# Layer norm of the second thousand tokens: features-by-tokens input in place of TensorE transposes

## The chip, the cores and the metric

One core of a Trainium2 chip runs the whole program. The metric is the device time of one execution in microseconds; the kernel before has a median of 2365.61 us over 3 runs (2364.18 to 2366.06). All tensors are float32.

## The reference

x has 2048 tokens of 1024 features. It is normalised over the features, xn = (x - mean) / sqrt(var + 1e-5), and xn feeds two branches. Branch A is linear attention with 32 heads of 32 features:

```python
xn = _layernorm(x, axis=-1)
s = _A_ref(xn, A_wqkv, A_w_phi, A_wo)      # softmax features, sums over the tokens, output product
g = _silu(_B_ref(xn, B_w1, B_w3, B_w2))    # silu(xn @ w1) * (xn @ w3) @ w2, 3584 hidden features
return x + s * g
```

TensorE sums over the partitions of both its operands, so every product with xn needs xn with features on the partitions, while mean and variance are per token and are easiest with tokens on the partitions.

## The kernel before, in words

**Products in three passes, seven for eight.** Every float32 operand is split into a high part (ScalarE casts, line 93) and a low part (VectorE subtracts, line 94), and a product takes three passes over the pairs. Blocks are multiplied by a scheme with seven products in place of eight: the activation operands are called A11, A12, A22, S1 to S4 (sums of blocks), the weight operands B11, B21, B22, T1 to T4.

**The stage in which the change lies.** The first stage multiplies w1 and w3 with the tokens: 28 column blocks of 128 features for the first 1024 tokens, then the same 28 for the second 1024 (loop over `seq`, lines 614 to 639). I call one of its products a step and number the steps as `seq` does: a step is 12 matmuls at line 627, and seven steps make a column block. Each step n does, in the order of the program: its matmuls; the weight sums on GpSimd that are due (lines 129 and 130, 553, 554); the split of the weight operand that step n+4 will need (ScalarE line 93, VectorE line 94, tile `bo`); whatever side work has been put at n (`after`); and then the eviction of its own result (`evict`, lines 563 to 592). Within this stage the five queues keep the program's order (`manual_schedule`), so that an instruction that waits holds all behind it on its queue.

**Evictions.** The seven steps of a block end in three PSUM banks' tags: `bankb` has three buffers, `banka` and `bankc` one each. In the single `bankc` S1 is started and copied out by ScalarE (line 576), S4 is added on top and evicted by VectorE (line 580, `wk<-bankc,wk`), and three steps later the next block's S1 starts in the same buffer: it can't start before that line 580 has ended. These steps are 84 (S4) and 87 (S1), 91 and 94, 98 and 101, and so on every seven.

**Side work.** Beside the steps the stage prepares what later stages need. `side_x` (four calls) makes the normalised operands of the second 1024 tokens, two 128-token tiles (a pair, numbers 4 to 7) at a time: it loads the two tiles with tokens on the partitions, takes mean and variance (`stats`, lines 193 to 196; `rstd`, 199 to 209), normalises them in place (`norm`, 211 to 214, VectorE), turns each of the four halves with four TensorE transposes (`turn`, 216 to 220), copies the turned half out of PSUM on ScalarE (`raw_x`, 222 to 225), forms the block sums on GpSimd (`a_sums`, 227 to 237), and splits and stores seven operands (`store_quad`, tiles `xoA` and `xoS`, DRAM tensors `xo_d1`). `side_fold` multiplies weight blocks by w_phi on TensorE (tile `pw`), `side_kv` prepares the weights of the key, value and query products (tiles `wkv`, `wkvo`), nine calls from step 69 on, 11 steps apart. Which step a piece stands at is worked out when the kernel is built: `room(step, cost)` goes on from a step until the VectorE time that the steps' own work and the pieces already placed there take stays within 2.4 us. GpSimd work isn't counted there. Side work that comes first takes its room first: `side_x`, then the folds, then `side_kv`.

**Queues.** All loads and stores of this stage are issued by SyncE (SP), in order.

Of the kernel before, what the change touches and what calls it, by code (L numbers as in the profile page):

```python
# [8 lines left out]
F = mybir.dt.float32  # L9
# [8 lines left out]
P = 128  # L18
NT = S // P
# [6 lines left out]


@with_exitstack
def tile_kernel(ctx: ExitStack, tc: tile.TileContext, x, wkT, wqT, wv, wphi, wo, w1, w3, w2, out):
    nc = tc.nc  # L30
    open_pools = {}

# [35 lines left out]
    dram = ctx.enter_context(tc.tile_pool(name="dram", bufs=1, space=DRAM))  # L68
# [15 lines left out]
    kv_d = [dram.tile([P, 8, DH], F, name=f"kv_d{c}") for c in range(2)]  # L84
    kvu_d = dram.tile([P, 16, DH], F, name="kvu_d")
    z_d = dram.tile([1, 2, 4, 4, 2, DH], F, name="z_d")


    PASSES = ((0, 0), (0, 1), (1, 0))
# [85 lines left out]
    def blk(name):  # L175
        return xp.tile([P, 4, P], F, name=name, tag="x")

    def flat(t):
        return t.rearrange("p k t -> p (k t)")
# [7 lines left out]
    def load_x(t, halves):  # L187
        for h in range(2):
            nc.sync.dma_start(halves[h], x[t * P:(t + 1) * P, h * 512:(h + 1) * 512])
        return halves  # L190

    def stats(mv, j, xt):
        st = small.tile([P, 2, 6], F, name="st")
        for a in range(2):
            nc.vector.bn_stats(st[:, a, :], xt[a])
        nc.vector.bn_aggr(mv[:, j], st.rearrange("p a b -> p (a b)"))

    def rstd(mv):

        sd = small.tile([P, 4, 2], F, name="sd")  # L200
        var = mv[:, :, 1]
        nc.scalar.activation(sd[:, 0], var, AF.Sqrt, bias=eps_t)
        nc.vector.reciprocal(sd[:, 1], sd[:, 0])

        nc.vector.tensor_mul(sd[:, 2], sd[:, 1], sd[:, 1])
        nc.vector.scalar_tensor_tensor(sd[:, 3], var, EPS, sd[:, 2], op0=OP.add, op1=OP.mult)
        nc.vector.tensor_scalar(sd[:, 3], sd[:, 3], -0.5, 1.5, op0=OP.mult, op1=OP.add)
        nc.vector.tensor_mul(sd[:, 1], sd[:, 1], sd[:, 3])
        return sd

    def norm(mv, sd, j, xt):

        for a in range(2):
            nc.vector.tensor_scalar(xt[a], xt[a], mv[:, j, 0:1], sd[:, 1, j:j + 1], op0=OP.subtract, op1=OP.mult)

    def turn(half):
        pt = ps.tile([P, 4, P], F, name="pt", tag="tr", bufs=3)
        for k in range(4):
            nc.tensor.transpose(pt[:, k, :], half[:, k * P:(k + 1) * P], ident)  # L219
        return pt  # L220

    def raw_x(pt):
        xf = blk("xf")
        nc.scalar.copy(xf, pt)
        return xf

    def a_sums(a, eng, part=None):

        if part in (None, 0):
            a["S3"] = blk("s3")  # L230
            eng.tensor_sub(flat(a["S3"]), flat(a["A11"]), flat(a["A21"]))
            a["S1"], a["S2"], a["S4"] = a["A21"], a["A11"], a["A12"]
            eng.tensor_add(flat(a["S1"]), flat(a["A21"]), flat(a["A22"]))
        if part in (None, 1):
            eng.tensor_sub(flat(a["S2"]), flat(a["S1"]), flat(a["A11"]))
        if part in (None, 2):
            eng.tensor_sub(flat(a["S4"]), flat(a["A12"]), flat(a["S2"]))
# [82 lines left out]
    for p in range(2):  # L320
        sd = rstd(mvs[p])
# [20 lines left out]
    for q in range(4):  # L342
        if q % 2 == 0:
            sd = rstd(mvs[2 + q // 2])
# [30 lines left out]
    before, after, rooms = {}, {}, []  # L375
# [10 lines left out]
    def at(step, f, d=after):  # L386
        d.setdefault(step, []).append(f)
# [4 lines left out]
    def room(step, cost):  # L392

        while True:
            f, j = divmod(step - 3, 7)
            base = (0.7, 0.7, 1.4, 1.4, 2.1, 0.7, 1.4 if f % 2 == 0 else 2.1)[j]
            if base + took.get(step, 0) + cost <= 2.4:
                took[step] = took.get(step, 0) + cost
                return step
            step += 1  # L400

    def store_quad(step, d, src, name):

        step = room(step, 1.0)

        def f():
            t = qp.tile(list(src().shape[:1]) + [2] + list(src().shape[1:]), R, name=name, tag="q")
            split(t[:, 0], t[:, 1], src())
            at(step + 2, lambda: nc.sync.dma_start(d, t.bitcast(F)))
        at(step, f)  # L410
        return step

    def side_x(i, s0):
        xt, a, mv, sd, pts = [], {}, [], [], {}
        t0, t1 = pairs[i]

        def load():
            xt.extend(load_x(t, [flat(blk("xt")) for _ in range(2)]) for t in (t0, t1))
            mv.append(small.tile([P, 2, 2], F, name="mv", bufs=4))

        at(s0, load)
        at_ = s0 + 2
        for j in range(2):
            at_ = room(at_ + 1, 1.6)
            at(at_, lambda j=j: stats(mv[0], j, xt[j]))
        at_ = room(at_ + 1, 1.0)
        at(at_, lambda: sd.append(rstd(mv[0])))
        for j in range(2):
            at_ = room(at_ + 1, 1.0)
            at(at_, lambda j=j: norm(mv[0], sd[0], j, xt[j]))  # L430
        s1 = at_ + 1
        for m, (n, j, hf) in enumerate((("A11", 0, 0), ("A12", 0, 1), ("A21", 1, 0), ("A22", 1, 1))):
            at(s1 + m, lambda n=n, j=j, hf=hf: pts.update({n: turn(xt[j][hf])}), before)
            at(s1 + m, lambda n=n: a.update({n: raw_x(pts[n])}))
        at_ = s1
        for n in ("A11", "A12"):
            at_ = store_quad(at_ + 1, xo_d[1][n][:, i - 4], lambda n=n: a[n], f"xo{n}")
        at_ = max(at_ + 1, s1 + 7)
        for m in range(3):
            at(at_ + m, lambda m=m: a_sums(a, nc.gpsimd, m))  # L440
        at_ += 1
        for n in ("S3", "S1", "S2", "S4", "A22"):
            at_ = store_quad(at_ + 1, xo_d[1][n][:, i - 4], lambda n=n: a[n], f"xo{n}")
# [59 lines left out]
    for i in range(4, 8):  # L503
        side_x(i, FIRST_STEP + 16 * (i - 4))
# [109 lines left out]
    for step, (k, an) in enumerate(seq):  # L614
        if step == 4:
            in_order(ENG.PE, ENG.Activation, ENG.DVE, ENG.Pool, ENG.SP)
        tb, f = divmod(k, NF)
# [6 lines left out]
        n = 0  # L624
# [477 lines left out]
    for r, new in enumerate(steps):  # L1102
        kb, i = new or (NKB, 0)
# [41 lines left out]
        if 26 <= r < 34:  # L1145
            c, a = (r - 26) // 4, (r - 26) % 4
            nc.sync.dma_start(zr_d[32 * a:32 * a + 32, c], z_d[:, c, a].rearrange("o j s f -> o (j s f)").to_broadcast([32, 256]))
        if 8 <= r < 24:
            c, j, s = (r - 8) // 8, (r - 8) // 2 % 4, r % 2
# [195 lines left out]
```

## Time and profile before

| what | value |
|---|---|
| median of 3 runs | 2365.61 us (2364.18 to 2366.06) |
| profiled execution, span | 2365.9 us (its own time is given by this span alone) |
| TensorE busy (PE) | 2337.4 us, 99% |
| VectorE busy (DVE) | 1753.2 us, 74% |
| ScalarE busy (ACT) | 859.2 us, 36% |
| GpSimd busy (POOL) | 760.5 us, 32% |
| DMA moved | 586.83 MB, mean 248 GB/s |

The profiled execution lies 0.3 us above the median, inside the spread of the runs. The shares are averages over stages; the stage of the change is the first half of the program, and the side work of `side_x` lies between 75 and 320 us. In the views of the timeline a line gives the start, the duration, the engine, the source line, the operation, the tile written and the tiles read, and, in brackets, the idle time ahead of it with what ended it.

### The profile page before, as it was taken

What the parts mean: (1) busy time and instruction counts of PE and PEld (TensorE: products, weight loads), DVE (VectorE), ACT (ScalarE), POOL (GpSimd) and SP (SyncE); (2) the same over time, 40 slices, a digit from 0 to 9 for tenths busy, and PEclk for the clock granted to TensorE, in tenths of its full rate; (3) what the DMA queues carried; (4) which work ended last, traced back from release to release, by engine and by line L of the source; (5) the groups of instructions that cost most, each with busy time, mean ns of one, the idle gap of its engine ahead of it and who ended that gap; (6) DMA issues with size and microseconds to landing.
All of it is one profiled execution on the core that took longest, in us unless ns stands there. A gap on an engine that the chain in (4) does not pass through costs nothing.

```text
span 2365.9 us, 35878 instructions
## 1 busy us (share of the span) xinstructions
PE 2337.4 (99%) x13298; PEld 1925.0 (81%) x13298; DVE 1753.2 (74%) x2539; ACT 859.2 (36%) x1534; POOL 760.5 (32%) x569
## 2 busy tenths in 40 slices
PE   6999999999999999999999999999999999999999
PEld 5888888888888888888888788888888888888877
DVE  8567788775688888885576555798688778888883
ACT  6445554443354445443232111234422222243100
POOL 1233555442355555552000000241011111115872
PEclk9999999999999999999999999999999999999999
DMA  7667689877887778776998877999445443377753
GB/s 262 202 216 237 230 292 309 286 249 226 260 279 261 257 264 281 261 267 218 372 341 323 326 240 256 350 351 333 154 137 179 178 178 111 125 254 289 250 186 132
DMA packets 319406, 586.83 MB, mean 248 GB/s; under 512 B 25600, under 2 KB 158208, under 8 KB 316544
## 3 DMA queue, kind: packets, MB, share of 16 engines
q1 hardware_dynamic: 304448, 569.87, 69.9%
q10 hardware_dynamic: 14784, 14.68, 1.8%
q8 instruction: 105, 1.72, 0.3%
q14 instruction: 69, 0.57, 0.1%
HBM read 379.19 MB, written 205.79 MB: 247 GB/s over the span
## 4 chain that ended last, share of the span: by engine, by line
PE 95%; DMA 2%; DVE 2%; SPq 1%; issue 1%; ACT 0%; POOL 0%; ACTq 0%; POOLq 0%; DVEq 0%
PE bankb L627 25%; PE bankb L1083 13%; PE bankc L627 12%; PE bankb L679 11%; PE pm L1210 7%; PE bankc L1083 6%; PE banka L627 6%; PE bankc L679 5%; PE banka L1083 3%; PE banka L679 3%; PE po L1054 1%; PE pkv L665 1%; PE pw L248 1%; SPq L166 0%; PE pt L219 0%
## 5 line engine op out<-in xcount | busy, mean ns | idle before, releaser
L94 DVE TENSOR_TENSOR bo<-rw,bo 128x512 fp32r<-128x512 f32 x336 | 307.7, 916 | 151.4 <-ACT bo L93 149.3
L1093 POOL TENSOR_TENSOR acc<-acc,u 128x512 f32<-128x512 f32 x48 | 63.4, 1321 | 449.1 <-ACT u L1092 434.3
L93 ACT CAST bo<-rw 128x512 fp32r<-128x512 f32 x336 | 201.1, 617 | 4.5 <-DMA w_d0T<-w2o 2.4
L1083 PE MATMUL bankb<-bo,as 128*128 128x512 f32 x816 | 200.7, 389 | 0.0
L1083 PEld LDWEIGHTS bankb<-bo,as 128*128 128x128 f32 x816 | 153.1, 188 | 31.9 <-DVE acc L1095 0.2
L1210 PE MATMUL pm<-wos,oT 128*128 128x512 f32 x720 | 166.9, 390 | 0.0
L627 PE MATMUL bankb<-op0A,bo 128*128 128x512 f32 x672 | 164.0, 391 | 0.1
L627 PE MATMUL bankb<-op0S,bo 128*128 128x512 f32 x672 | 163.2, 391 | 0.0
L627 PE MATMUL bankc<-op0S,bo 128*128 128x512 f32 x672 | 162.9, 391 | 0.0
L627 PE MATMUL bankc<-op1S,bo 128*128 128x512 f32 x672 | 161.5, 389 | 1.0 <-ACT bo L93 1.0
L627 PE MATMUL bankb<-op1S,bo 128*128 128x512 f32 x672 | 161.6, 389 | 0.1
L627 PE MATMUL bankb<-op1A,bo 128*128 128x512 f32 x672 | 161.4, 389 | 0.0
L1210 PEld LDWEIGHTS pm<-wos,oT 128*128 128x128 f32 x720 | 134.6, 188 | 30.6 <-issue 2.9
L627 PEld LDWEIGHTS bankc<-op1S,bo 128*128 128x128 f32 x672 | 126.0, 188 | 27.6 <-ACT bo L93 1.4
L627 PEld LDWEIGHTS bankb<-op1S,bo 128*128 128x128 f32 x672 | 126.0, 188 | 26.7 <-ACT h L569 0.6
L627 PEld LDWEIGHTS bankb<-op1A,bo 128*128 128x128 f32 x672 | 126.1, 188 | 26.2
L627 PEld LDWEIGHTS bankb<-op0S,bo 128*128 128x128 f32 x672 | 125.6, 188 | 25.6
L627 PEld LDWEIGHTS bankc<-op0S,bo 128*128 128x128 f32 x672 | 125.5, 188 | 25.7
L627 PEld LDWEIGHTS bankb<-op0A,bo 128*128 128x128 f32 x672 | 125.4, 188 | 25.8 <-DVE op0A L94 0.4
L1083 PE MATMUL bankc<-bo,as 128*128 128x512 f32 x576 | 146.1, 389 | 0.0
L1095 DVE TENSOR_TENSOR acc<-bankb,acc 128x512 f32<-128x512 f32 x152 | 104.3, 686 | 30.8 <-PE bankb L1083 26.6
L1083 PEld LDWEIGHTS bankc<-bo,as 128*128 128x128 f32 x576 | 108.1, 188 | 22.4
(246 smaller groups left out, 4686.7 us busy)
## 6 DMA issues: line engine op xcount, KB each, us to landing
rw<-in_w SPq DMA_DIRECT2D x224, 256.0 KB, 3.5
hr<-h_d SPq DMA_DIRECT2D x56, 512.0 KB, 4.1
xoS<-xo_d0S SPq DMA_DIRECT2D x48, 512.0 KB, 8.7
xoS<-xo_d1S SPq DMA_DIRECT2D x48, 512.0 KB, 6.6
xoA<-xo_d0A SPq DMA_DIRECT2D x36, 512.0 KB, 7.2
xoA<-xo_d1A SPq DMA_DIRECT2D x36, 512.0 KB, 6.2
e<-e_d SPq DMA_DIRECT2D x32, 512.0 KB, 5.6
h_d<-h SPq DMA_DIRECT2D x56, 256.0 KB, 4.0
```

The costliest lines, as they stand in the source:

```text
L93: nc.scalar.copy(hi, src)
L94: (by or nc.vector).tensor_sub(lo, src, hi.bitcast(F))
L248: nc.tensor.matmul(pw[:, g, :], wr[:, g], bd[:, 4 * c + g, :], start=True, stop=True)
L627: nc.tensor.matmul(bank, bt[:, w, kk], aos[tb][an][:, u, kk], start=an in ("A11", "A12", "S1") and n == 0, stop=LAST[b] == an and n == 11, ...
L665: nc.tensor.matmul(pkv[sl, m], e[:, m // 4, (m % 4) * P + 32 * h:(m % 4) * P + 32 * h + 32], v[:, 4 * (m % 4) + h], start=first and m == 0 ...
L679: nc.tensor.matmul(bank[b], xo[an][:, u, k], wb[bn][:, w, k], start=an in ("A11", "A12", "S1") and n == 0, stop=LAST[b] == an and n == 11, ...
L1054: nc.tensor.matmul(po[a][32 * j:32 * j + 32, 256 * c:256 * c + 256], kvt[sl, c, j, s], ets[c, j // 2][sl, 2 * (j % 2) + s].rearrange("p t ...
L1083: nc.tensor.matmul(bank[b], t[:, u, pos + k], bos[kb, bn, k][:, w], start=first and n == 0, stop=LAST[b] == an and n == 5, skip_group_chec ...
L1093: nc.gpsimd.tensor_add(c, c, u)
L1095: nc.vector.tensor_add(c, pb, c)
L1210: nc.tensor.matmul(p, oT[a][k // 4][:, u, k % 4], wos[c, 4 * (k % 2) + k // 2][:, w], start=n == 0, stop=n == 23)
```

## The change

For pairs 4 to 7 x is given to the kernel a second time, laid out by the host as an input `xT` with features on the partitions (for each of the 8 tiles of 128 tokens, 128 partitions of 2 x 4 x 128 numbers). The tokens-by-features load and the statistics stay. Normalising and turning are replaced: mean and factor of the pair are put side by side in `mv`, stored to DRAM as four rows of 128 numbers (`st_d`), read back to all 128 partitions (`rows`, 2 KB each), and four blocks of `xT` are loaded straight into the tiles that `raw_x` filled before. GpSimd subtracts the mean row from each (`centre`), VectorE multiplies by the factor row (`scale_x`). `norm`, `turn` and `raw_x` aren't called for these pairs any more. The first 1024 tokens are as before.

```diff
-        xt, a, mv, sd, pts = [], {}, [], [], {}
+        xt, a, mv, sd, rows = [], {}, [], [], []
         t0, t1 = pairs[i]
+        d = st_d[i - 4]
...
-        at(at_, lambda: sd.append(rstd(mv[0])))
-        for j in range(2):
-            at_ = room(at_ + 1, 1.0)
-            at(at_, lambda j=j: norm(mv[0], sd[0], j, xt[j]))
-        s1 = at_ + 1
-        for m, (n, j, hf) in enumerate((("A11", 0, 0), ("A12", 0, 1), ("A21", 1, 0), ("A22", 1, 1))):
-            at(s1 + m, lambda n=n, j=j, hf=hf: pts.update({n: turn(xt[j][hf])}), before)
-            at(s1 + m, lambda n=n: a.update({n: raw_x(pts[n])}))
-        at_ = s1
+
+        def root():
+            sd.append(rstd(mv[0]))
+            nc.vector.tensor_copy(mv[0][:, :, 1], sd[0][:, 1])
+
+        at(at_, root)
+        at(at_ + 1, lambda: nc.sync.dma_start(d.rearrange("o j m p -> p (o j m)"), mv[0].rearrange("p j m -> p (j m)")))
+
+        def load_t():
+            rows.append(blk("rows"))
+            nc.sync.dma_start(flat(rows[0]), d.rearrange("o j m p -> o (j m p)").to_broadcast([P, 512]))
+            for n, t, hf in (("A11", t0, 0), ("A12", t0, 1), ("A21", t1, 0), ("A22", t1, 1)):
+                a[n] = blk("xf")
+                nc.sync.dma_start(flat(a[n]), xT[t - NT // 2][:, hf].rearrange("p k t -> p (k t)"))
+
+        at(at_ + 4, load_t)
+        s1 = at_ + 7
+        for m, (n, j) in enumerate((("A11", 0), ("A12", 0), ("A21", 1), ("A22", 1))):
+
+            def centre(n=n, j=j):
+                nc.gpsimd.tensor_sub(a[n], a[n], rows[0][:, 2 * j].unsqueeze(1).to_broadcast([P, 4, P]))
+
+            def scale_x(n=n, j=j):
+                nc.vector.tensor_mul(a[n], a[n], rows[0][:, 2 * j + 1].unsqueeze(1).to_broadcast([P, 4, P]))
+
+            at(s1 + m, centre)
+            at_ = room(max(at_ + 1, s1 + m + 1), 0.7)
+            at(at_, scale_x)
+        s1 = at_ - 3
```

The pieces that follow (splits, sums, stores of the pair) move with it, and the pieces of `side_kv`, which take the room that is left, move as well. By the rules of `room` pair 7 has its last split at step 99 in place of step 90. Source lines after the added ones are higher in the new kernel: line 94 is 95 there, 580 is 602, 553 and 554 are 575 and 576, 129 to 130 are 130 to 131.

On VectorE, the 12 rows from the eviction of step 84 on. In these rows `bo` is the split for a later step, `xoS` a stored operand of pair 7, `wkvo` one of `side_kv`, `wk`, `h` the step's own evictions. Before:

```order
L580 TENSOR_TENSOR wk_851<-bankc,wk_851 128x512
L581 TENSOR_TENSOR h_855<-h_855,wk_851 128x512
L94 TENSOR_TENSOR bo<-rw,bo 128x512
L94 TENSOR_TENSOR xoS_2907<-s_2833,xoS_2907 128x512
L94 TENSOR_TENSOR bo<-rw,bo 128x512
L585 TENSOR_TENSOR wk_850<-wk_850,wk_852 128x512
L589 TENSOR_TENSOR wk_849<-wk_849,wk_850 128x512
L94 TENSOR_TENSOR bo<-rw,bo 128x512
L94 TENSOR_TENSOR xoS_2949<-xf,xoS_2949 128x512
L94 TENSOR_TENSOR bo<-wk_853,bo 128x512
L94 TENSOR_TENSOR xoS_2971<-xf,xoS_2971 128x512
L94 TENSOR_TENSOR bo<-rw,bo 128x512
```

The same place in the new kernel, where `xf<-xf,rows` is `scale_x`:

```order
L602 TENSOR_TENSOR wk_855<-bankc,wk_855 128x512
L603 TENSOR_TENSOR h_859<-h_859,wk_855 128x512
L95 TENSOR_TENSOR bo<-rw,bo 128x512
L452 TENSOR_TENSOR xf<-xf,rows 128x512
L95 TENSOR_TENSOR wkvo<-wkv,wkvo 128x512
L95 TENSOR_TENSOR bo<-rw,bo 128x512
L607 TENSOR_TENSOR wk_854<-wk_854,wk_856 128x512
L611 TENSOR_TENSOR wk_853<-wk_853,wk_854 128x512
L95 TENSOR_TENSOR bo<-rw,bo 128x512
L452 TENSOR_TENSOR xf<-xf,rows 128x512
L95 TENSOR_TENSOR wkvo<-wkv,wkvo 128x512
L95 TENSOR_TENSOR bo<-wk_857,bo 128x512
```

Two `scale_x` and two pieces of `side_kv` stand where three splits of pair 7 stood; the splits come later. From the eviction of step 84 to that of step 98 VectorE has 36 instructions before (the latter counted) and 39 now.

On GpSimd, the rows about the weight sums of steps 77 to 91. `rw` and `wk` are the weight sums of the steps, `wkv` those of `side_kv`, `s` and `xf` the sums of pair 7. Before, the four sums of pair 7 lie about the weight sums of step 84 (the first lines 129 and 130 here) and ahead of the eviction of that step:

```order
L554 TENSOR_TENSOR rw<-rw,wk_853 128x512
L231 TENSOR_TENSOR s_2833<-xf 128x512
L233 TENSOR_TENSOR xf<-xf 128x512
L235 TENSOR_TENSOR xf<-xf 128x512
L129 TENSOR_TENSOR rw<-rw 128x512
L130 TENSOR_TENSOR wk_853<-rw 128x512
L237 TENSOR_TENSOR xf<-xf 128x512
L129 TENSOR_TENSOR wkv<-wkv 128x512
L130 TENSOR_TENSOR wkv<-wkv 128x512
L553 TENSOR_TENSOR rw<-rw,wk_853 128x512
L554 TENSOR_TENSOR rw<-rw,wk_853 128x512
```

Now four `centre` (`xf<-xf,rows`) are there, and the four sums of pair 7 come one block of weight sums later:

```order
L576 TENSOR_TENSOR rw<-rw,wk_857 128x512
L449 TENSOR_TENSOR xf<-xf,rows 128x512 x2
L130 TENSOR_TENSOR rw<-rw 128x512
L131 TENSOR_TENSOR wk_857<-rw 128x512
L449 TENSOR_TENSOR xf<-xf,rows 128x512
L130 TENSOR_TENSOR wkv<-wkv 128x512
L131 TENSOR_TENSOR wkv<-wkv 128x512
L575 TENSOR_TENSOR rw<-rw,wk_857 128x512
L449 TENSOR_TENSOR xf<-xf,rows 128x512
L576 TENSOR_TENSOR rw<-rw,wk_857 128x512
L482 TENSOR_TENSOR wkv<-wkv 128x512
L484 TENSOR_TENSOR wkv<-wkv 128x512
```

From the first weight subtraction behind the eviction of step 84 (line 553, now 575) up to the pair of weight sums that stands at step 98, GpSimd has 12 instructions before and 17 now: one `centre` and four sums of pair 7 more.

On SP, the rows of pair 4 in the new kernel: the store of the statistics, and behind a few weight loads the read-back and the four loads of `xT`. `wr<-in_wqT` is the load of a fold.

```order
L435 DMA st_d_257<-mv 128x4x1
L492 DMA wq_d_6_144<-wr 128x512
L242 DMA wr<-in_wqT 128x512
L258 DMA rw<-in_w 128x512
L521 DMA xo_d0A_87<-op0A_302 128x8x128
L258 DMA rw<-in_w 128x512
L439 DMA rows<-st_d_257 128x512
L442 DMA xf<-in_xT 128x512 x4
L541 DMA h_d_0_57<-h_859 128x4x128
L258 DMA rw<-in_w 128x512
```

The read-back waits for the store to land, and what stands behind it on SP waits with it.

More of the change, by code (lines that the diff above doesn't have):

```diff
@@ L28, in tile_kernel @@
 @with_exitstack
-def tile_kernel(ctx: ExitStack, tc: tile.TileContext, x, wkT, wqT, wv, wphi, wo, w1, w3, w2, out):
+def tile_kernel(ctx: ExitStack, tc: tile.TileContext, x, xT, wkT, wqT, wv, wphi, wo, w1, w3, w2, out):
     nc = tc.nc
@@ L86, in tile_kernel @@
     z_d = dram.tile([1, 2, 4, 4, 2, DH], F, name="z_d")
+    st_d = [dram.tile([1, 2, 2, P], F, name=f"st_d{i}") for i in range(4)]
     PASSES = ((0, 0), (0, 1), (1, 0))
@@ L1323 @@
         "x": np.asarray(A_x).reshape(S, D),
+        "xT": np.asarray(A_x).reshape(NT, P, 2, 4, P)[NT // 2:].transpose(0, 4, 2, 3, 1),
         "wkT": lay(wqkv[:, D:2 * D]),
```

## The prediction

> **What bounds the kernel now.** I read the page first, then the busy times by stretch, then the timelines of TensorE, VectorE and GpSimd where the side work is densest.
>
> ```profile
> span 2365.9 us, 35878 instructions
> PE 2337.4 (99%) x13298; PEld 1925.0 (81%) x13298; DVE 1753.2 (74%) x2539; ACT 859.2 (36%) x1534; POOL 760.5 (32%) x569
> ```
>
> TensorE is busy 99% of the span, so what it no longer has to do is gained, if nothing else becomes late. Whether something does is read in the stage itself. The busy times by stretch (TensorE, weight loads, VectorE, ScalarE, GpSimd, granted clock, DMA share, GB/s):
>
> ```profile
> core 0: us, PE busy (x) PEld busy (x) DVE busy (x) ACT busy (x) POOL busy (x), PEclk, DMA share, GB/s
> 100.00:140.00 40.00, 40.00 (x197) 33.50 (x196) 25.62 (x31) 18.95 (x36) 16.02 (x11) 1.00 0.68 215
> 180.00:220.00 40.00, 40.00 (x190) 33.42 (x189) 33.16 (x46) 20.25 (x36) 17.63 (x12) 1.00 0.59 193
> 260.00:300.00 40.00, 40.00 (x185) 33.06 (x185) 31.67 (x41) 22.37 (x39) 20.99 (x15) 1.00 0.79 270
> 300.00:340.00 40.00, 40.00 (x178) 33.11 (x178) 36.50 (x41) 18.84 (x35) 24.27 (x16) 1.00 0.89 307
> ```
>
> TensorE never stands still from 100 us on, at full clock. VectorE has room at 100 us (25.62 of 40) and little at 300 us (36.50 of 40), where the work of pair 7 meets that of `side_kv`. That place decides the forecast.
>
> **What the transposes cost.** TensorE's timeline at two of the 16 groups of four transposes:
>
> ```profile
> 107.47 0.60 PE L219 MATMUL pt<-ident,xt 128*128 128x128 f32 x4
> 107.82 3.00 PE L627 MATMUL bankb<-op0A,bo 128*128 128x512 f32 x12
> 110.66 0.60 PE L219 MATMUL pt<-ident,xt 128*128 128x128 f32 x4
> 111.02 3.02 PE L627 MATMUL bankb<-op0S,bo 128*128 128x512 f32 x12
> 113.87 2.88 PE L627 MATMUL banka<-op0A,bo 128*128 128x512 f32 x12
> 116.59 2.88 PE L627 MATMUL bankc<-op0S,bo 128*128 128x512 f32 x12
> ```
>
> A step without transposes lasts 116.59 - 113.87 = 2.72 us. With a group ahead it lasts 110.66 - 107.47 = 3.19 and 113.87 - 110.66 = 3.21: a group costs 0.48 us, the slower first matmuls behind it included. There are 4 pairs x 4 halves = 16 groups (64 transposes), all on the path, since TensorE is never idle there: 16 x 0.48 = **7.7 us gained on TensorE**.
>
> **What else goes and comes, off the path.** The groups of instructions between 90 and 300 us, by line:
>
> ```profile
> L224 ACT COPY xf<-pt 128x512 f32<-128x512 f32 x16 | 9.4, 588 | 4.4 <-PE pt L219 4.4
> L214 DVE TENSOR_SCALAR xt<-xt,mv,sd 128x512 f32<-128x512 f32 x16 | 8.9, 599 | 0.0
> L231 POOL TENSOR_TENSOR s<-xf 128x512 f32<-128x512 f32 x4 | 6.5, 1630 | 0.0
> ```
>
> ScalarE loses the 16 copies, 9.4 us; at about half busy it isn't waited for, so I count nothing. VectorE loses 16 `norm` instructions (8.9 us) and gets 16 `scale_x` and four copies of two elements a partition. GpSimd gets 16 `centre`, of the shape of line 231, at about 1.6 us each: 26 us on an engine that is half idle here. By themselves these would cost nothing; together they don't stay apart, as the next views show.
>
> VectorE's timeline, rows between 298 and 313 us, and GpSimd's beside them:
>
> ```profile
> 298.69 1.78 DVE L94 TENSOR_TENSOR bo<-rw,bo 128x512 fp32r<-128x512 f32 x1
> 300.38 1.77 DVE L94 TENSOR_TENSOR wkvo<-wkv,wkvo 128x512 fp32r<-128x512 f32 x1
> 302.08 0.68 DVE L578 TENSOR_TENSOR wk<-bankb,wk 128x512 f32<-128x512 f32 x1
> ...
> 307.98 0.68 DVE L580 TENSOR_TENSOR wk<-bankc,wk 128x512 f32<-128x512 f32 x1
> ...
> 309.91 0.68 DVE L94 TENSOR_TENSOR bo<-rw,bo 128x512 fp32r<-128x512 f32 x1
> 310.51 0.68 DVE L94 TENSOR_TENSOR xoS<-s,xoS 128x512 fp32r<-128x512 f32 x1
> 311.21 0.69 DVE L94 TENSOR_TENSOR bo<-rw,bo 128x512 fp32r<-128x512 f32 x1
> ```
>
> ```profile
> 298.18 1.73 POOL L129 TENSOR_TENSOR rw<-rw 128x512 f32<-128x512 f32 x1
> 299.99 1.62 POOL L130 TENSOR_TENSOR wk<-rw 128x512 f32<-128x512 f32 x1
> 301.57 1.74 POOL L237 TENSOR_TENSOR xf<-xf 128x512 f32<-128x512 f32 x1
> ...
> 308.14 1.29 POOL L553 TENSOR_TENSOR rw<-rw,wk 128x512 f32<-128x512 f32 x1 [1.42 <-DVE bo L94]
> ```
>
> The same subtraction of line 94 starts every 0.60 us while GpSimd rests (309.91, 310.51) and every 1.70 us while GpSimd works (298.69, 300.38). Line 578, with one source in PSUM, takes 0.68 us even then. So a GpSimd instruction can cost VectorE up to 1.70 - 0.60 = 1.10 us, if VectorE has work with both sources in SBUF to do, and `scale_x` is such work, 0.60 or 1.70 us.
>
> How close that is to the path is seen at `bankc`: TensorE's products in it, and then VectorE's eviction from it two blocks later:
>
> ```profile
> 300.96 2.88 PE L627 MATMUL bankc<-op0S,bo 128*128 128x512 f32 x12
> ...
> 309.12 2.88 PE L627 MATMUL bankc<-op0S,bo 128*128 128x512 f32 x12
> ...
> 347.20 2.88 PE L627 MATMUL bankc<-op0S,bo 128*128 128x512 f32 x12
> ```
>
> ```profile
> 343.98 0.68 DVE L580 TENSOR_TENSOR wk<-bankc,wk 128x512 f32<-128x512 f32 x1
> ```
>
> Step 84 starts at 300.96, and its line 580 ends at 307.98 + 0.68 = 308.66. Step 87, which needs the bank, starts at 309.12: VectorE is only **0.46 us** ahead of TensorE. At step 98 the line ends at 344.66 and step 101 starts at 347.20: 2.54 us ahead. Between the two VectorE recovered 2.1 us in 14 steps (38.1 us).
>
> The same 36.0 us as one stretch, VectorE and then GpSimd:
>
> ```profile
> 308.70:344.70 36.00, 32.51 (x37) 1.00 0.93 324
> ```
>
> ```profile
> 308.70:344.70 36.00, 18.57 (x13) 1.00 0.93 324
> ```
>
> The order has 36 VectorE instructions there: 36 x 0.60 = 21.6 us without contention, 32.51 us were taken. The other 10.9 us, shared among GpSimd's 12 instructions, are 0.91 us for each.
>
> Now the change. By the order VectorE has 39 instructions between the two evictions, 3 more: 1.8 us. GpSimd has 17 in place of 12, one `centre` and the four sums of pair 7 more: 5 x 0.91 to 5 x 1.10 = 4.5 to 5.5 us. Together 6.3 to 7.3 us, against the 2.54 us that were spare: 3.8 to 4.8 us by which line 602 (the old 580) would be late, and TensorE waits for it at steps 94 to 101. On the other side the order has about one GpSimd instruction fewer in the solid run ahead of step 84, up to 1.1 us, so 2.7 to 4.8 us; I take the middle, **3.7 us given back**. The row nearest to this wait is the 0.46 us: no wait of this kind is in the trace of before, so its size rests on this sum alone.
>
> [...]
>
> Ahead of step 84, in pairs 4 to 6, VectorE has 33.16 of 40 us at most, and I count no stall; the bound is another 3.7 us if the overlapping pairs 5 and 6, whose 8 `centre` and 8 scalings fall between steps 46 and 59 by the rule of `room`, do the same there.
>
> **The sum.** 2365.9 - 7.7 + 3.7 = **2361.9 us**, made against the profiled execution (2365.9, 0.3 above the median of the runs, which is less than the runs differ).
>
> **New transfers.** Each pair adds six issues on SP: the store of the statistics, the read-back and four blocks. 20 of the 24 move 256 KB. The rows of comparable transfers, with the median time to landing last:
>
> ```profile
> xt<-in_x SPq DMA_DIRECT2D x32, 256.0 KB, 5.2
> wr<-in_wqT SPq DMA_DIRECT2D x16, 256.0 KB, 4.3
> zr_d<-z_d SPq DMA_DIRECT2D x8, 32.0 KB, 7.8
> ```
>
> The blocks are issued three steps (8.2 us) ahead of `centre`; 5.2 us hides in that. The store writes 512 single numbers; the nearest small transfer landed in 7.8 us, and the read-back stands three steps (8.2 us) behind it, so I count nothing. Bounds: 0, and the second rival below. The stores of pair 7 end nine steps later; their reader is the second half of the stage, some 80 steps on, so that delay costs nothing.
>
> **Rivals.** *The whole gain stays*: VectorE absorbs the extra work, because it recovered 2.1 us in that stretch and has 4 us idle in 40. Then 2365.9 - 7.7 = 2358.2. Against it speaks the 0.46 us. It holds if the extra work costs VectorE under 2.5 us in place of 6.3 to 7.3.
>
> *The store of the statistics lands late and SP stands still*: the read-back waits for it, and behind it wait the weight loads and the load of the next fold. A fold's load is issued four steps (10.9 us) ahead of its matmuls and lands in 4.3, so 6.6 us are spare. TensorE begins to wait when the store takes over 8.2 + 6.6 = 14.8 us to land. At 20 us that is 5.2 us for each of pairs 4 to 6, where folds still run: 2361.9 + 15.6 = 2377.5, slower than before. For it: single numbers of 4 bytes, which no transfer of the trace has. Against it: 7.8 us in the nearest row. [...]
>
> *The contention hurts twice*: pairs 5 and 6 give back the same 3.7 us, and the whole comes to 2361.9 + 3.7 = 2365.6, no change.
>
> **How the numbers follow.** A difference of 0.2% (4.7 us: under 2360.9 or over 2370.3) is about what a measurement here can tell from none. Forecast, 2361.9 with 2360.9 to 2363.0 from its own terms: 0.50. Whole gain: 0.25. Contention twice: 0.15. SP held: 0.10. The forecast's lower edge and the whole gain lie under 2360.9: faster 0.28. SP held and a part of contention twice at larger prices lie over 2370.3: slower 0.12. The rest, 0.60, is no change that can be told. The range takes in the whole gain, set against the median (2365.6 - 7.7 = 2357.9), and the double contention with its upper bound (1.1 us more in either stretch): 2357.9 to 2367.8.
>
> **What would show it.** Right: in the new profile line 219 has no rows after 90 us; the waits of TensorE show `bankc` waiting for VectorE's line 602, or `bo` for line 95, some 3 to 4 us in all between 300 and 360 us; steps with no transposes last 2.72 us throughout. Wrong: no such wait (whole gain), waits of `pw` for `wr` with SP held at `rows` (the store), or waits at steps 49 to 63. A granted clock under 1.00 in this stage would make all of it void.

## The result and the profile after

| kernel | median, us | runs |
|---|---|---|
| before | 2365.84 | 2364.18 to 2366.23 (4) |
| changed | 2392.27 | 2390.55 to 2393.73 (4) |

The changed kernel takes 1.0113 times as long [1.0101, 1.0125]: it is slower by 26.4 us, where I had forecast 2361.9 and a range of 2357.9 to 2367.8. The profiled execution took 2390.55 us, 1.75 more than its span; spans are compared with spans below. The page's head after the change:

```profile
span 2388.8 us, 35792 instructions
PE 2334.6 (98%) x13234; PEld 1920.4 (80%) x13234; DVE 1774.0 (74%) x2543; ACT 850.9 (36%) x1518; POOL 787.3 (33%) x585
```

The span grew by 22.9 us. TensorE's busy time fell by 2.8 (2337.4 to 2334.6), so its idle time grew by 25.7. The loss is idle TensorE, in a stretch where it had not stood still (before, its only wait of the stage behind 75 us is one of 1.0 us at 615.4). The busy times by stretch, columns as before (TensorE, weight loads, VectorE, ScalarE, GpSimd, granted clock, DMA share, GB/s):

```profile
core 0: us, PE busy (x) PEld busy (x) DVE busy (x) ACT busy (x) POOL busy (x), PEclk, DMA share, GB/s
100.00:140.00 40.00, 36.00 (x156) 30.00 (x156) 20.03 (x26) 13.02 (x24) 15.69 (x12) 0.91 0.73 223
180.00:220.00 40.00, 36.64 (x171) 30.33 (x170) 28.48 (x40) 16.36 (x28) 17.78 (x13) 1.00 0.72 201
220.00:260.00 40.00, 28.96 (x124) 23.91 (x123) 25.36 (x29) 13.49 (x25) 18.27 (x13) 0.87 0.63 214
300.00:340.00 40.00, 37.06 (x163) 30.07 (x161) 29.51 (x31) 16.14 (x30) 21.73 (x14) 1.00 0.86 250
340.00:380.00 40.00, 34.03 (x141) 26.92 (x140) 37.46 (x38) 17.79 (x34) 23.88 (x15) 0.96 0.81 275
```

Only the last two rows lie where I had expected a loss. The first three lie earlier, in stretches where VectorE and GpSimd have room. What TensorE waited for (sum in us, times, longest):

```profile
PE pw L249 <- DMA wr<-in_wqT: 19.1, 6, 11.0
PE bankc L649 <- DVE wk L602: 6.1, 3, 2.9
PE bankb L649 <- DVE wk L600: 1.7, 2, 1.2
PE bankb L649 <- ACT h L591: 1.1, 1, 1.1
```

The first row is new: before, the same wait came to 1.1 us. It is the fold's matmuls (`pw`) waiting for their weight block `wr`. The other three, 8.9 us together, all lie between 316 and 373 us; 7.8 of them are waits for VectorE, 1.1 is one for ScalarE. TensorE's timeline shows the first and the largest of the fold's waits, in brackets:

```profile
104.12 2.05 PE L249 MATMUL pw<-bd,wr 128*128 128x128 f32 x8 [4.00 <-DMA wr<-in_wqT]
105.82 4.82 PE L649 MATMUL bankc<-op0S,bo 128*128 128x512 f32 x12
110.48 2.90 PE L649 MATMUL bankb<-op0A,bo 128*128 128x512 f32 x12
...
115.94 2.88 PE L649 MATMUL banka<-op0A,bo 128*128 128x512 f32 x12
118.66 2.88 PE L649 MATMUL bankc<-op0S,bo 128*128 128x512 f32 x12
...
242.27 2.04 PE L249 MATMUL pw<-bd,wr 128*128 128x128 f32 x8 [11.04 <-DMA wr<-in_wqT]
243.97 4.06 PE L649 MATMUL bankc<-op0S,bo 128*128 128x512 f32 x12
```

With a third one of 3.36 us at 196.5 these are 18.4 of the 19.1 us. The transposes are gone, and steps last 118.66 - 115.94 = 2.72 us as forecast. But after a wait the product that follows is slow: 4.82 and 4.06 us in place of 2.88.

**Why the first fold waits.** SP's own queue (start, duration of the issue), and the DMA traffic from 88 to 106 us, in slots of 0.45 us (busy tenths, GB/s), with the last number of an issue's row its time from issue to landing:

```profile
90.49 0.38 SPq L435 DMA_DIRECT2D st_d<-mv  x1
...
91.47 0.42 SPq L242 DMA_DIRECT2D wr<-in_wqT  x1
```

```profile
DMA  0005930349100000311141060102590697999999
GB/s 0 0 0 82 346 141 14 3 102 419 64 0 0 0 0 0 27 41 5 18 27 18 9 18 5 9 0 23 23 36 5 127 191 185 349 366 343 366 366 358
wr<-in_wqT SPq DMA_DIRECT2D x1, 256.0 KB, 12.5
st_d<-mv SPq DMA_DIRECT2D x1, 2.0 KB, 10.0
```

The store of the statistics (2 KB as 512 numbers of 4 bytes) landed after 10.0 us. The weight block behind it was issued in good time, 1 us later, but from 93 to 102 us almost nothing moves (0 to 41 GB/s), and it landed after 12.5 us. Before, in the same stretch, it took 3.6:

```profile
wr<-in_wqT SPq DMA_DIRECT2D x1, 256.0 KB, 3.6
```

At the second fold SP itself stands: it holds the read-back `rows` until the store of 176.42 has landed, and issues the fold's block only 4.5 us after that. What SP waited for at the read-back (`L439`; sum, times, longest, the longest here) stands below the rows.

```profile
176.42 0.38 SPq L435 DMA_DIRECT2D st_d<-mv  x1
...
186.08 0.33 SPq L439 DMA_DIRECT2D rows<-st_d  x1
...
190.58 0.52 SPq L242 DMA_DIRECT2D wr<-in_wqT  x1
```

```profile
SPq L439 <- DMA st_d<-mv: 13.2, 3, 7.5
```

**Why the third fold waits 11 us.** SP's queue again, and the VectorE row at which it goes on:

```profile
223.18 12.19 SPq L190 DMA_DIRECT2D xt<-in_x  x4
...
238.94 0.33 SPq L242 DMA_DIRECT2D wr<-in_wqT  x1
```

```profile
234.33 0.68 DVE L95 TENSOR_TENSOR xoS<-s,xoS 128x512 fp32r<-128x512 f32 x1
```

No slow transfer is at work here: the fold's block landed 3.2 us after its issue at 238.94. Loading pair 7 takes four buffers from the one set of 14 that the 128x512 blocks of x share with the blocks of the folds (`wr`) and `rows`. In the kernel before the same four issues took 2.69 us:

```profile
216.23 2.69 SPq L189 DMA_DIRECT2D xt<-in_x  x4
```

Now the fourth is free only when VectorE has split a sum of pair 5 at 234.33. SP keeps its order, so the fold's load stands behind that, and then 3.0 us more for a buffer of its own, which the store `wq_d` of the fold before gives back when it lands:

```profile
SPq L190 <- DVE xoS L95: 10.4, 1, 10.4
SPq L242 <- DMA wq_d<-wr: 3.0, 1, 3.0
```

Two things moved here: a pair now takes ten such buffers, nine before (`rows` is the tenth), and pair 5's splits come later, since `scale_x` takes room ahead of them. No run separates the two.

### The profile page after: what moved, and what is told of

It is laid out like the page before. It is cut to its first block, busy times and chain, and to the rows that moved or that the text cites. A ratio compares the mean times of both kernels' runs of the same rounds, so it can differ in the third digit from the quotient of the medians.

```text
span 2388.8 us, 35792 instructions
## 1 busy us (share of the span) xinstructions
PE 2334.6 (98%) x13234; PEld 1920.4 (80%) x13234; DVE 1774.0 (74%) x2543; ACT 850.9 (36%) x1518; POOL 787.3 (33%) x585
## 4 chain that ended last, share of the span: by engine, by line
PE 89%; DMA 4%; DVE 4%; issue 1%; ACT 1%; SPq 0%; POOL 0%; ACTq 0%; DVEq 0%; POOLq 0%
PE bankb L649 22%; PE bankb L1105 13%; PE bankc L649 12%; PE bankb L701 10%; PE pm L1232 7%; PE bankc L1105 6%; PE banka L649 5%; PE bankc L701 5%; PE banka L1105 3%; PE banka L701 3%; DMA wr<-in_wqT 1%; PE po L1076 1%; PE pkv L687 1%; DVE bo L95 1%; DMA xo_d1A<-xoA 1%
## 5 line engine op out<-in xcount | busy, mean ns | idle before, releaser
L95 DVE TENSOR_TENSOR bo<-rw,bo 128x512 fp32r<-128x512 f32 x336 | 316.3, 942 | 161.7 <-ACT bo L94 161.1
L649 PEld LDWEIGHTS bankb<-op0S,bo 128*128 128x128 f32 x672 | 125.7, 188 | 27.3 <-ACT h L591 1.5
```

The costliest lines, as they stand in the source:

```text
L95: (by or nc.vector).tensor_sub(lo, src, hi.bitcast(F))
L649: nc.tensor.matmul(bank, bt[:, w, kk], aos[tb][an][:, u, kk], start=an in ("A11", "A12", "S1") and n == 0, stop=LAST[b] == an and n == 11, ...
```

## The experiments

My theory after this result was that three separate things had happened: the 4-byte store clogs the queue behind it; pair 7's early load has no buffer and blocks SP; and VectorE and GpSimd contend about 320 us, as forecast. The rivals were that the 20 extra loads, not the store, made the transfers late, and that the later waits only follow from the earlier ones.

**The store alone, on the kernel before.** Nothing reads what it stores.

```diff
         at(at_, lambda: sd.append(rstd(mv[0])))
+        at(at_ + 1, lambda: nc.sync.dma_start(st_d[i - 4].rearrange("o j m p -> p (o j m)"), mv[0].rearrange("p j m -> p (j m)")))
```

> The kernel before, with the store of the statistics (512 single numbers, four times) added and nothing else; what is stored is mean and variance, and nobody reads it. Theory A, the store itself stops the transfers behind it on its queue for about 10 us: a fold whose weights are loaded right behind a store is late, TensorE waits about 4 us at each of one or two folds, 2369.5 to 2375 us. Rival B, the extra 5 MB of loads and read-backs crowd the transfers and the store is harmless: 2365.6 to 2366.6 us.

Measured: 2370.34 us median (2367.74 to 2374.36, 10 runs) against 2365.28, ratio 1.0021 [1.0012, 1.0031]. The landing (smallest, median, largest; the profile has it for the third of the four stores alone, issued at 197.49), and the traffic from 88 to 106 us, about the first store:

```profile
DMA to landing us min/median/max: 9.4/9.4/9.4
```

```profile
DMA  0000005999984236464708143842876999999964
GB/s 0 0 0 0 0 0 59 323 240 320 155 18 14 9 9 59 27 27 27 23 14 32 9 18 18 50 9 27 191 105 233 354 348 349 356 405 361 315 191 68
```

With no other transfer added, the traffic falls from 320 to between 9 and 59 GB/s from 93 to 100 us, much as in the changed kernel. The extra loads aren't needed for it. That the profiled execution lost little (its span is 2365.7) is a matter of timing: it is the fastest of the ten, and the first fold's block just escaped; a later one waited 1.65 us at 210.7.

**The same store in pieces of 16 bytes**, 128 in place of 512, again unread.

```diff
-st_d[i - 4].rearrange("o j m p -> p (o j m)"), mv[0]...
+st_d[i - 4].rearrange("o j m p -> (o j m p)").rearrange("(p n) -> p n", n=4), mv[0]...
```

> The run with the store alone, but the four numbers of a partition are stored side by side, 128 pieces of 16 bytes in place of 512 of 4. If the number of pieces that share a stretch of DRAM is what holds the transfers, landing falls well under 9.4 us, to 2 to 5 us; if any piece under some size does it, it stays at 8 to 10 us.

One run, 2368.33 us, which tells no difference in time by itself. The landing (again of the third store alone) and the traffic (90 to 106 us, slots of 0.4 us) do:

```profile
DMA to landing us min/median/max: 3.0/3.0/3.0
```

```profile
DMA  0000000059899900069589999731004749973000
GB/s 0 0 0 0 0 0 0 0 164 323 244 370 205 61 5 0 26 169 184 138 289 380 352 349 325 223 100 29 0 0 77 148 133 307 325 216 78 10 24 22
```

3.0 us in place of 9.4, and 1.6 us of low traffic in place of 7. That there was work to move is seen at the 512 KB store issued 3.0 us behind the first store of the statistics, with the 4-byte pieces and then with those of 16 bytes (landing last; 4.4 in the kernel before):

```profile
xo_d0A<-op0A SPq DMA_DIRECT2D x1, 512.0 KB, 11.4
xo_d0A<-op0A SPq DMA_DIRECT2D x1, 512.0 KB, 5.7
```

So the same 2 KB in pieces of 16 bytes do little harm; the 512 pieces of 4 bytes do. Whether their number or their size does it, no run separates.

**The statistics turned before they are stored.** In the changed kernel one TensorE transpose a pair turns mean and factor, ScalarE copies them, and four rows of 512 bytes are stored; the read-back stands a step later.

```diff
-        at(at_ + 1, lambda: nc.sync.dma_start(d.rearrange("o j m p -> p (o j m)"), mv[0]...
+        at(at_ + 2, turn_stats, before)
+        at(at_ + 2, copy_stats)
+        at(at_ + 3, lambda: nc.sync.dma_start(d.rearrange("o j m p -> (o j m) p"), mt[0]))
...
-        at(at_ + 4, load_t)
+        at(at_ + 5, load_t)
```

> The changed kernel, with the statistics turned by one TensorE transpose per pair and stored as four rows of 512 bytes, the read-back one step later. Theory A: the waits of 4.4 and 3.8 us at the first two folds go, that of 11.4 us at the fold of step 59 stays, because a buffer causes it: 2380 to 2386 us. Rival B: no better than 2391 us. Rival C, the late store alone causes all three waits: 2370 to 2375 us.

Measured: 2382.71 us (2379.83 to 2383.8), ratio to before 1.0068 [1.0053, 1.0083]. The landing of the read-backs (the profile has two of the four and none of the stores; the first store had landed at most 4.1 us after its issue, when SP issued its read-back without a wait), and what TensorE waited for:

```profile
DMA to landing us min/median/max: 3.8/4.8/5.7
```

```profile
PE pw L249 <- DMA wr<-in_wqT: 12.1, 1, 12.1
...
PE bankc L661 <- DVE wk L614: 2.9, 1, 2.9
PE bankb L661 <- DVE wk L612: 1.9, 1, 1.9
```

The first two waits of the folds are gone and the third, of the buffer, stays whole: two causes. For the first fold the place of the store changed as well as its form: its load is issued at 91.63 now, ahead of the store at 96.36. Two later loads of folds were issued 0.8 us behind a turned store and landed after 3.7 and 3.9 us, where 12.5 were measured behind the 4-byte store. And the waits about 320 us fell from 8.9 to 4.8 us, which I hadn't looked for: part of them hung on the store too, as far as one profile of each tells.

**Pair 7's load later.** The changed kernel, with pair 7's x loaded at step 61 in place of 55.

```diff
-        at(s0, load)
+        at(s0 + 6 * (i == 7), load)
```

> The changed kernel, with the load of x of pair 7 six steps later (61 in place of 55) and nothing else. Theory D, that load waits on its queue for one of the 14 block buffers, held until the split of pair 5 at step 57, and the load of a fold waits behind it: the wait of 11.4 us goes, 2379 to 2383 us. Rival C, the late store causes that wait: 2390 to 2394 us.

Measured: 2382.37 us (2381.46 to 2382.64), ratio 1.0067 [1.0052, 1.0082]. TensorE has no wait between 220 and 260 us any more, so the 11 us were the buffer's; the two waits at the earlier folds stay (the first is 4.09 us), and the waits about 320 us still sum to 8.6 (2.6 of them for ScalarE).

**Both.** The last two edits together.

> Both edits of the two runs before. Theory A with D and the contention of VectorE and GpSimd about steps 87 to 104 as a third cause of its own: the waits for folds go, some 8 to 10 us of waits for VectorE stay, 2367 to 2374 us. Rival E, those waits for VectorE are only the late transfers' after-effect: 2357 to 2361 us.

Measured: 2370.75 us (2367.62 to 2373.37, 10 runs), ratio 1.0018 [1.0009, 1.0028]. Of the medians, the store's cure saves 9.6 us alone, the later load 9.9, both 21.5: they add up within 2 us. What is left in the stage:

```profile
PE pw L249 <- DMA wr<-in_wqT: 4.6, 5, 2.4
PE bankc L661 <- DVE wk L614: 4.2, 2, 2.9
...
PE bankb L661 <- DVE wk L612: 0.3, 1, 0.3
```

One fold still waits 2.4 us, at 243. The waits for VectorE are 4.5 us, half of the 8 to 10 that I expected of this run, against 3.7 (2.7 to 4.8) in the forecast. Whether they come from what the forecast named is the next question.

**Without GpSimd's work on pair 7.** The last kernel, with pair 7's four `centre` and four sums left out (what is left out is told in the expectation).

```diff
-            at(s1 + m, centre)
+            if i < 7:
+                at(s1 + m, centre)
...
-            at(at_ + m, lambda m=m: a_sums(a, nc.gpsimd, m))
+            if i < 7:
+                at(at_ + m, lambda m=m: a_sums(a, nc.gpsimd, m))
+            elif m == 0:
+                at(at_ + m, no_sums)
```

> The run with turned statistics and the later load, with GpSimd's eight instructions of pair 7 left out (its mean is not subtracted and its block sums are not formed, the splits take the unsummed blocks). Theory H, GpSimd's instructions take VectorE's time: the waits of 5 us about steps 94 to 104 fall under 1 us, 2363 to 2367 us. Rival I, the three more VectorE instructions there do it alone: the waits stay at 4 to 5 us, 2369 to 2372 us.

Measured: 2364.58 us (2362.79 to 2367.17, 10 runs), 0.9996 of before [0.9987, 1.0005]. TensorE's waits for VectorE and for the fold's block:

```profile
PE pw L249 <- DMA wr<-in_wqT: 2.2, 1, 2.2
...
PE bankc L668 <- DVE wk L621: 0.8, 1, 0.8
```

4.5 us fell to 0.8, with VectorE's work the same. Eight GpSimd instructions were worth 3.7 us of TensorE's waiting, which is the contention of the forecast. A rival would be that VectorE had stood waiting for GpSimd's results. The traces rule it out: from 270 to 355 us VectorE has no wait for GpSimd in either run, but between the evictions of steps 91 and 98 it takes 349.69 - 326.91 = 22.78 us with GpSimd's work and 343.70 - 325.79 = 17.91 without, for the same 18 instructions. The fold's wait hardly moved, as it should.

**The pieces of `side_kv` later.** If two streams of side work collide, moving one apart should do what leaving work out did. On the kernel with both cures:

```diff
-        side_kv(m // 4, m % 4, FIRST_STEP + 62 + 11 * m)
+        side_kv(m // 4, m % 4, FIRST_STEP + 69 + 10 * m)
```

> The changed kernel with statistics turned by TensorE, the load of pair 7 six steps later, and the nine pieces of side_kv starting at step 76, ten steps apart, in place of step 69, eleven apart. Theory F, the waits about steps 94 to 104 come from pair 7 meeting the first pieces of side_kv on VectorE and GpSimd: they go or fall under 1 us, 2362 to 2367 us with the one late fold that is left. Rival G, VectorE's own load in this stage is too high wherever the pieces stand: waits of 4 us and more come up elsewhere, 2369 to 2373 us.

Measured: 2366.87 us (2362.57 to 2372.17, 11 runs), 1.0005 of before [0.9996, 1.0014]. `bankc` now waits 1.6 us for VectorE in place of 4.2, not quite the fall under 1 us that I expected; the time is in the range of theory F. The fold's wait about 242 us stays (2.67).

**And the folds' matmuls two steps further behind their load** (six steps in place of four, the store of the result two later).

```diff
-        at(s0 + 4, lambda: w.append(flat(fold(w[0], c))), before)
-        at(s0 + 4, lambda: nc.scalar.copy(flat(w[0]), w[1]))
-        at(s0 + 6, lambda: nc.sync.dma_start(d, flat(w[0])))
+        at(s0 + 6, lambda: w.append(flat(fold(w[0], c))), before)
+        at(s0 + 6, lambda: nc.scalar.copy(flat(w[0]), w[1]))
+        at(s0 + 8, lambda: nc.sync.dma_start(d, flat(w[0])))
```

> The run before, with the matmuls of each fold six steps behind the load of its weights in place of four. If the remaining waits for folds are only that load's distance, they go and TensorE's gain of 7.7 us is left whole: 2357 to 2361 us, faster than both kernels. If waits for VectorE remain, 2362 to 2367 us.

Measured: 2362.47 us (2359.3 to 2364.71, 11 runs), 0.9983 of before [0.9974, 0.9992]. This version beats both kernels, by 3.3 us and some 30 us, but stays above the 2357 to 2361 us that a whole gain would have given. Its page's head, and the stretch of the third fold:

```profile
span 2360.7 us, 35802 instructions
PE 2328.9 (99%) x13238; PEld 1915.6 (81%) x13238; DVE 1782.0 (75%) x2543; ACT 851.6 (36%) x1522; POOL 790.5 (33%) x585
```

```profile
220.00:260.00 40.00, 40.00 (x187) 33.39 (x186) 35.40 (x43) 19.97 (x38) 21.76 (x15) 1.00 0.79 263
```

TensorE is busy there at full clock again. Its busy time over the span is 2337.4 - 2328.9 = 8.5 us below that of before, but not all of it comes from the transposes: with the store alone, which keeps all 64, it was 2334.9. From the start of step 15 to that of step 130, where all 64 lie, TensorE is busy for 322.2 us in place of 328.6, so they were worth 6.4 us there, with four small transposes for the statistics and the restarts after waits already taken off. Of the waits 1.65 us are left in these steps, 1.4 of them at `bankc`; and at 604 and 611 us TensorE waits 2.3 us in all, 1.0 before. That takes 3.0 of the 6.4 us and leaves 3.4, about the 3.3 of the medians.

**The two moves without the change**, as a control: `side_kv` and the folds moved as above in the kernel before, all 64 transposes kept.

> The kernel before with the two moves of the best version alone: the pieces of the key, value and query weights begin at step 69 + 7 (10 apart), and the fold's matmuls stand six steps behind its load instead of four. No features-by-tokens load, no store of statistics, all 64 transposes stay. If the gain of the best version (0.9983 of the kernel before, 3.3 us) comes from the transposes that went, these moves alone are worth nothing, since TensorE has no wait in the stage before: ratio 0.9993 to 1.0010. If the gain came from the moves themselves, whatever is done to x, the ratio is 0.9975 to 0.9990.

Measured: 2365.76 us (2363.13 to 2367.45, 11 runs) against 2365.42, ratio 1.0000 [0.9991, 1.0009]. So the gain of the best version comes from the transposes; the moves only let it through.

## Why the prediction was wrong, step by step

**TensorE's gain: right.** 16 groups at 0.48 us were forecast as 7.7 us; from step 15 to step 130 the busy time of the best version shows 6.4, net of what came new there.

**Contention at `bankc`: right in place and cause, near in size.** Forecast: line 602 late at steps 94 to 101, 3.7 us. With the store and the load cured the waits for VectorE are 4.5 us, at steps 94, 100 and 101, and 3.7 of them go with GpSimd's work on pair 7. That the two 3.7 agree is luck: the forecast counted three VectorE and five GpSimd instructions more, while the run left VectorE's in and took eight of GpSimd's out. The 0.12 for slower counted on larger prices of the contention as well; no run shows those. In the changed kernel itself the waits there are 8.9 us, those for ScalarE included; the 4.1 to 4.4 more (8.9 and 8.6 with the 4-byte store, 4.8 and 4.5 without) hung on the store. By which transfer each came I can't say in full. One part is seen: `centre` stands idle for its loads (idle time of GpSimd last)

```profile
L449 POOL TENSOR_TENSOR xf<-xf,rows 128x512 f32<-128x512 f32 x16 | 23.6, 1484 | 18.8 <-DMA xf<-in_xT 18.8
```

for 18.8 us over the four pairs, and with it the weight sums behind it on GpSimd. With turned statistics that is 13.5. So "5.2 us hides in that", the line on the blocks, was wrong too: three steps didn't cover the landing of blocks that SP issued late.

**The new transfers: this is the step that failed.** "The store writes 512 single numbers; the nearest small transfer landed in 7.8 us, and the read-back stands three steps (8.2 us) behind it, so I count nothing." The landing was 9.4 to 10.0 us, not far off. What failed is that I asked only who reads the store's result, and not what shares its queue. In place of nothing, two folds lost 4.00 + 3.36 us by it, and the waits about 320 us another 4, as far as single profiles tell. The rival with SP held had the right culprit and the wrong condition. It let TensorE wait only for a landing over 14.8 us. At the first fold the load stood not behind a standing SP but in a clogged queue, and the 4.3 us that I took as given for it were 12.5. At the second fold SP did stand, but the 8.2 us that I put between store and read-back weren't there: SP reached the read-back 2.2 us after the store's issue (176.42 to 178.57), stood 7.5 us, and the fold's load was late with a landing of at most 9.7. I gave the rival 0.10.

**The buffers: missing from the same term.** The largest single wait, 11.04 us, came from a count that the prediction doesn't have; the new transfers' zero covered it too. The order of the new kernel shows which instruction is behind which, but not that a load at step 55 needs a buffer that is free after step 57. Nothing in the timing of before hinted at it: there this load took 2.69 us to issue, and TensorE stood nowhere near it.

**The clock: named as what would void the forecast, and not priced.** The rows above show it at 0.91, 0.87 and 0.96 in three of the five stretches shown. The product behind the wait of 4.00 us took 110.48 - 105.82 = 4.66 us, 1.94 over the usual 2.72; after 11.04 us the next took 3.90, 1.18 over. From the start of step 15 to that of step 130 TensorE's busy time is 329.2 - 322.2 = 7.0 us above that of the best version, which runs the same products at full clock: slow matmuls, and a little for the restarts after more waits. For these steps the whole is +27.3 us of idle time, -6.4 of transposes, +7.0 of slow matmuls: 27.9, from 328.6 to 356.5 us. The spans differ by less, 22.9, because the profiled execution of before was slower elsewhere (next paragraph); the medians differ by 26.4.

**The base.** I set a span against a median of runs. Wherever both are known, a run's own time is 1.7 to 2.3 us over its span (2390.55 and 2388.8; 2367.45 and 2365.2). So the profiled execution of before, with a span of 2365.9, was some 2 us slower than the median run, not 0.3, and that the base came out near the median is luck. It changes nothing in the verdict.

## What to carry to other kernels

Before adding a small transfer to a queue, look at the two or three transfers behind it, not only at its reader, and at the pieces it is cut into: here 2 KB turned with one transpose and stored as four rows of 512 bytes gave 2382.71 us, stored as single numbers 2392.27. Where loads take buffers from a shared set, list for every load that moves, or whose set gets one more user, which instruction frees its buffer and what waits behind the load on its queue. And when work is taken off a busy engine, the moves that keep the others on time are part of the change: with the turned store, the later load and the two moves of other pieces, leaving out the 64 transposes won 3.3 us; without them it lost 26. In the kernel before, the two moves were worth nothing alone.

## What the runs showed of the hardware that I had not expected

A store of 512 pieces of 4 bytes landed after 9.4 to 10.0 us, where the landing is on record, and while it did what was behind it on SP's queue moved at 0 to 59 GB/s for 7 to 9 us, where 343 to 405 are seen behind that. In 128 pieces of 16 bytes it landed after 3.0 us, and in four rows of 512 bytes after at most 4.1 the first time, so 16 bytes landed about as soon as 512. Why the pieces of 4 bytes hold up what is behind them stays open.

After some waits of TensorE its clock was lower for a few microseconds: in the changed kernel it was 0.50 from 104 to 107 us, behind the wait of 4.00, and 1.00 from 111. The rows about a shorter wait:

```profile
343.42 2.97 PE L649 MATMUL bankb<-op0A,bo 128*128 128x512 f32 x12 [1.22 <-DVE wk L600]
349.28 4.31 PE L649 MATMUL bankc<-op0S,bo 128*128 128x512 f32 x12 [2.90 <-DVE wk L602]
353.43 2.89 PE L649 MATMUL bankb<-op0A,bo 128*128 128x512 f32 x12
```

Behind the wait of 1.22 us the product took 2.97 us, hardly more than the usual 2.88; the one behind 2.90 us cost 353.43 - 349.28 - 2.72 = 1.43 us more, with the clock at 0.61 from 349 to 353. Behind the wait of 11.04 us the clock was 0.50 as well (242 to 246 us). Behind that of 3.36 us, at 196.53, there was no drop: the clock was 1.00 from 196 to 200, and the next product took 2.99 us. With turned statistics the product behind a wait of 2.88 us, at 339.62, took 3.00 us, and one behind only 1.87 us, at 358.11, took 4.58, with the clock at 0.60 from 358 to 360. So here the length of a wait alone didn't decide.
